# Attention and feed-forward on one Trainium2 core: the first stage and first chunk in one written order, scores taken from the loaded keys, block sums in column quarters

## The chip, the cores and the metric

The kernel runs on one core of a Trainium2 chip. The core has five engines that run side by side: PE (TensorE, matrix multiplications), DVE (VectorE), ACT (ScalarE), POOL (GpSimd) and SP, which here only issues transfers (DMA). The metric is device microseconds of one launch. The median of three runs before is 675.34 us (675.28 to 675.90).

## The reference

```python
# q, k, v: (4 batches, 8 heads, 768 positions, 64), fp32; w_in, w_out arrive as 64-bit floats
k_sum = k.reshape(B, H, 24, 32, D).max(axis=3)          # maxima of blocks of 32
v_sum = v.reshape(B, H, 24, 32, D).mean(axis=3)         # means of blocks of 32
scores_l = where(|i - j| < 16, scale * q @ k.T, -1e9)   # a band around the diagonal
scores_s = scale * q @ k_sum.T + log(32)
a = softmax(concat(scores_l, scores_s))
x = (a @ concat(v, v_sum)).reshape(B * S, H * D)        # 3072 x 512
h = x @ w_in                                            # 512 -> 2048
out = where(h > 0, h, exp(min(h, 0)) - 1) @ w_out       # 2048 -> 512
```

## The kernel before

Two heads make a pair, so there are four pairs of each batch. A "unit" is 256 positions (four windows of 64 queries) of one pair. A window sees 96 keys and 24 block maxima, so its scores are 128 x 120: 64 queries of each of two heads. For each unit PE makes the scores (`unit_scores`, L386), DVE adds the mask and finds the row minimum of the negated scores (L118), ACT takes the exponentials (L122), DVE makes the reciprocal of the sum (L124, L125), POOL multiplies (L126), PE transposes (L132), ACT or DVE copies the result (L133), PE multiplies with the values (L139), and `take_x` splits the result into a rounded part `xh` (ACT, L152) and the rest `xl` (DVE, L153).

The feed-forward part takes chunks of 512 positions, six in all, and runs 96 iterations n: chunk c = n // 16, slice f = n % 16 of the 2048 hidden columns. `layer1` (L412) makes `h` from twelve products; ACT takes exp (L415), DVE makes the ELU (L416, L417), ACT rounds it to `gh` (L420), POOL makes the rest `gl` (L421); `layer2` (L432) of iteration n is issued in iteration n + 1. Iterations n = 0 to 79 also carry 40 units, one for two iterations: an even n has the scores of the next unit and the transposes of the present one, an odd n its values. In the first chunk scores, transposes and values share one PSUM bank, "a0".

The weights are 32 tiles, (1, f) of w_in and (2, f) of w_out, 512 KB each as 64-bit floats. Each is turned into two fp32 tiles by `convert`: POOL shifts the low words (L98), ACT scales the high words into PSUM (L96), DVE joins them (L100, L103), ACT rounds (L106), POOL subtracts (L107).

The first stage, `first_units`, makes the first chunk's x: 512 positions of all four pairs. It loads q as blocks with zeros (`q_t`) and k whole (`kn`), copies the windows of k and its maxima into `k_t`, and multiplies full 128 x 128 tiles (L289). The block means of v come from twelve products with 512 columns (L298). A scheduler orders the first stage on PE, DVE, ACT and POOL; only SP is written by hand there. In the loop PE and SP are written by hand, and the scheduler places the rest. Six weights are converted ahead of the loop, two more in each iteration of the first chunk. For the next batch, `summary` loads k and v of a whole pair (`n`, 384 KB) and reduces them on DVE (L361); `means` (L376) is eight products.

SP keeps at most eight transfers open: the ninth waits for the first. `load_unit` issues six transfers of 40 to 144 KB (L322, L328, L332, L340, L341).

## Time and profile before

| | |
|---|---|
| median of three runs | 675.34 us |
| the profiled execution | 675.21 us |
| its span, first to last instruction | 673.4 us |
| PE busy | 649.0 us, 96% of the span |
| DVE, ACT, POOL busy | 274.5, 280.2, 249.4 us |
| chain that ended last | PE 85%, DMA 6%, POOL 3% |

The busy times are sums over the span. What matters for a change at the start is the start alone, so the views of the first 105 us are read apart from the rest: the timeline of PE (when an iteration's first `layer1` starts), the groups of instructions in one window (count, mean, idle time before and what ended it), and the windows view (busy time, granted clock and bytes moved in each stretch).

### The profile page before, as it was taken

The page shows a single profiled execution, that of the slowest core. Times are in us where ns is not written, and L with a number is a line of the kernel's source. Part 1 is how long each engine was busy: PE and PEld are TensorE (multiplying, and loading weights), DVE is VectorE, ACT ScalarE, POOL GpSimd, SP SyncE. Part 2 cuts the span into 40 slices and gives each one's busy share as a digit, 9 for nine tenths or more (in the row PEclk, how much of TensorE's full clock was granted, in tenths as well). Part 3 has the DMA queues.
Part 4 walks back from the last instruction along what each step waited for, and adds up shares of the span by engine and source line. Part 5 has one row for each costly group of instructions (what it writes and reads, how often), then busy time and mean ns, then how long its engine had stood idle before and what let it go on. Part 6 is the DMA issues. An engine that isn't in the chain of part 4 may idle for free.

```text
span 673.4 us, 10291 instructions
## 1 busy us (share of the span) xinstructions
PE 649.0 (96%) x3688; PEld 527.6 (78%) x3688; DVE 274.5 (41%) x866; ACT 280.2 (42%) x754; POOL 249.4 (37%) x269
## 2 busy tenths in 40 slices
PE   7769999999999999999999999999999999999996
PEld 5457777888888888888888888888888888888885
DVE  6676987772333543222322553232322222311111
ACT  5565666674334334433433433343434333322222
POOL 7466787983223222322222232223223222122221
PEclk9969999999999999999999999999999999999999
DMA  9979982113112341411212443112312100100001
GB/s 293 303 192 323 336 277 70 36 46 96 47 32 79 100 131 41 126 32 32 58 36 55 137 128 79 47 43 55 94 32 60 32 1 1 63 0 1 0 1 63
DMA packets 88146, 60.21 MB, mean 89 GB/s; under 512 B 48544, under 2 KB 80544, under 8 KB 88096
## 3 DMA queue, kind: packets, MB, share of 16 engines
q1 hardware_dynamic: 84784, 53.66, 28.8%
q10 hardware_dynamic: 3312, 5.90, 2.4%
q8 instruction: 29, 0.48, 0.3%
q14 instruction: 21, 0.17, 0.1%
HBM read 52.46 MB, written 6.29 MB: 87 GB/s over the span
## 4 chain that ended last, share of the span: by engine, by line
PE 85%; DMA 6%; POOL 3%; SPq 2%; DVE 1%; ACT 1%; issue 1%; ACTq 0%; POOLq 0%
PE h L412 37%; PE o L432 37%; PE s L386 5%; DMA raw_w<-in_w_out_dram 4%; PE o_ps L139 3%; PE t_ps L132 2%; DMA v<-in_v_dram 1%; DMA raw_w<-in_w_in_dram 1%; POOL raw_w L98 1%; POOL w L107 1%; ACT sm L122 1%; SPq L158 1%; POOL gl L421 1%; POOL sm L126 0%; SPq L250 0%
## 5 line engine op out<-in xcount | busy, mean ns | idle before, releaser
L412 PE MATMUL h<-xh,w 128*128 128x512 f32 x768 | 262.0, 402 | 1.5 <-ACT xh L152 1.5
L421 POOL TENSOR_TENSOR gl<-e,gh 128x512 fp32r<-128x512 f32 x96 | 123.7, 1289 | 206.3 <-issue 114.0
L432 PE MATMUL o<-w,gh 128*128 128x512 f32 x768 | 196.1, 394 | 0.0
L412 PEld LDWEIGHTS h<-xh,w 128*128 128x128 f32 x768 | 144.6, 188 | 33.1 <-ACT xh L152 1.7
L432 PEld LDWEIGHTS o<-w,gh 128*128 128x128 f32 x768 | 141.2, 188 | 27.8 <-DVE ot L453 0.4
L416 DVE TENSOR_SCALAR e<-e 128x512 f32<-128x512 f32 x96 | 49.2, 512 | 260.6 <-ACT e L415 260.6
L412 PE MATMUL h<-xl,w 128*128 128x512 f32 x384 | 150.3, 391 | 0.3 <-DVE xl L153 0.3
L415 ACT ACTIVATE e<-h 128x512 f32<-128x512 f32 x96 | 57.3, 597 | 205.0 <-PE h L412 204.8
L126 POOL TENSOR_TENSOR sm<-sm,z 128x480 f32<-128x480 f32 x48 | 48.1, 1003 | 161.7 <-ACT gh L420 130.1
L432 PE MATMUL o<-w,gl 128*128 128x512 f32 x384 | 105.4, 389 | 0.0
L420 ACT CAST gh<-e 128x512 fp32r<-128x512 f32 x96 | 59.0, 614 | 67.3 <-DVE e L417 65.9
L122 ACT ACTIVATE sm<-sm,mx 128x120 f32<-128x120 f32 x192 | 73.6, 385 | 30.9 <-DVE mx L118 28.2
L432 PEld LDWEIGHTS o<-w,gl 128*128 128x128 f32 x384 | 72.0, 188 | 15.2 <-POOL gl L421 0.2
L412 PEld LDWEIGHTS h<-xl,w 128*128 128x128 f32 x384 | 72.5, 189 | 13.3 <-DVE xl L153 0.6
L417 DVE SCALAR_TENSOR_TENSOR e<-h,e 128x512 f32<-128x512 f32 x96 | 66.1, 689 | 1.9
L107 POOL TENSOR_TENSOR w<-cv,w 128x512 fp32r<-128x512 f32 x32 | 42.0, 1321 | 12.1 <-ACT w L106 11.4
L386 PEld LDWEIGHTS s<-kw,qbd 128*128 128x128 f32 x320 | 42.5, 194 | 5.0 <-DVE xl L153 2.0
L386 PE MATMUL s<-kw,qbd 128*128 128x120 f32 x320 | 43.0, 278 | 1.6 <-DVE xl L153 1.6
L118 DVE CUSTOM_DVE_ANT_0 sm<-s,mask 128x120 f32<-128x120 f32 x192 | 42.5, 277 | 4.5 <-PE s L289 3.3
L153 DVE TENSOR_TENSOR xl<-o_ps,xh 128x256 fp32r<-128x256 f32 x48 | 20.0, 422 | 56.6 <-ACT xh L152 56.5
L122 ACT ACTIVATION_READ_ACCUMULATOR sm<-sm,mx 128x1 f32 x192 | 36.1, 188 | 0.0
L133 ACT COPY pt<-t_ps 120x512 f32<-120x512 f32 x44 | 25.7, 585 | 22.6 <-PE t_ps L132 22.2
(69 smaller groups left out, 390.1 us busy)
## 6 DMA issues: line engine op xcount, KB each, us to landing
raw_w<-in_w_in_dram SPq DMA_DIRECT2D x16, 512.0 KB, 6.6
raw_w<-in_w_out_dram SPq DMA_DIRECT2D x16, 512.0 KB, 8.4
qbd<-in_qT_dram SPq DMA_DIRECT2D x80, 64.0 KB, 2.3
out_dram<-ot ACTq DMA_DIRECT2D x20, 256.0 KB, 3.8
kw<-in_kT_dram SPq DMA_DIRECT2D x28, 144.0 KB
vw<-in_v_dram SPq DMA_DIRECT2D x28, 144.0 KB, 3.5
n<-in_kT_dram SPq DMA_DIRECT2D x16, 192.0 KB, 2.5
n<-in_vT_dram SPq DMA_DIRECT2D x16, 192.0 KB, 2.5
```

The lines of the kernel that those rows point to most:

```text
L107: nc.gpsimd.tensor_tensor(out=w[:, 1, :], in0=cv, in1=w[:, 0, :].bitcast(F32), op=ALU.subtract)
L118: low = nc.vector.tensor_tensor_reduce(out=sm[:, t, :], in0=s_ps[:, t, :], in1=m, scale=-scale, scalar=3.0e38, op0=ALU.add, op1=ALU.min, a ...
L122: exp = nc.scalar.activation(out=sm[:, t, :], in_=sm[:, t, :], func=AF.Exp, bias=mx[:, t, :], scale=-1.0, accum_out=z[:, t, :])
L126: mul = nc.gpsimd.tensor_tensor(out=sm, in0=sm, in1=z.broadcast_to([P, UW, KC]), op=ALU.mult)
L386: nc.tensor.matmul(s_ps[:, t, :], qbd[u % 2][:, t, :], kw[p][:, t, :], start=True, stop=True)
L412: nc.tensor.matmul(h_ps, w[:, a, cols], bb[:, cc, :], start=(k == 0), stop=(k == 3 * NCC - 1))
L415: exp = nc.scalar.activation(out=e, in_=h_ps, func=AF.Exp)
L416: nc.vector.tensor_scalar(out=e, in0=e, scalar1=1.0, scalar2=-1.0, op0=ALU.min, op1=ALU.add)
L417: elu = nc.vector.scalar_tensor_tensor(out=e, in0=h_ps, scalar=0.0, in1=e, op0=ALU.max, op1=ALU.add)
L420: nc.scalar.copy(out=gh, in_=e)
L421: low = nc.gpsimd.tensor_tensor(out=gl, in0=e, in1=gh.bitcast(F32), op=ALU.subtract)
L432: nc.tensor.matmul(o_acc[c][s], a[:, s * P:(s + 1) * P], w[:, bb, :], start=first and f == 0, stop=last and f == NF - 1)
```

## The change

Scores of the first stage no longer need the blocks `q_t` and `k_t`: each head of each window is one product of 64 x 64 queries with 96 keys straight from `kn`, and one with 24 maxima from `ks`; the two heads of a pair stand in the two halves of the rows and of the output. That is 32 products for a pair in place of 8. The block sums become 24 products of 128 columns, each pair in its own quarter of the output columns of PE (`tile_position=(0, p * BLK)`), and `means` likewise. The first stage and the first sixteen iterations stand in one written order on all five engines. `convert` becomes a generator of four parts (POOL; ACT; DVE; ACT and POOL) that are called half an iteration apart; three weights are converted in the first stage, two in each iteration after it. The weights are loaded in the order of their use, and the loads of units 0 and 1 stand between weights. Summaries are loaded in one iteration and reduced in the next, at a fixed place. From the second chunk on the scheduler places DVE, ACT and POOL as before.

```diff
+    order = [(1, 0)]
+    for f in range(1, NF):
+        order += [(1, f), (2, f - 1)]
+    order.append((2, NF - 1))
+    todo, loads = list(order), list(order)
...
-    def convert(key, turn):
...
+    def convert(tag="a1"):
...
+        key = todo.pop(0)
...
-        sh = psum.tile([P, WC], F32, tag="a1", name="sh")
+        nc.gpsimd.tensor_scalar(out=lo_w, in0=lo_w.bitcast(U8)[:, :, 3], scalar1=1 / 32, scalar2=-31 / 64,
+                                op0=ALU.mult, op1=ALU.add)
+        yield
+        sh = psum.tile([P, WC], F32, tag=tag, name="sh")
         bits = sh.bitcast(U32)
-        with tc.issue_after(turn[1]):
-            nc.scalar.mul(out=sh, in_=hi_w.bitcast(F32), mul=2.0 ** -112)
-        with tc.issue_after(turn[2]):
-            nc.gpsimd.tensor_scalar(out=lo_w, in0=lo_w.bitcast(U8)[:, :, 3], scalar1=1 / 32, scalar2=-31 / 64,
-                                    op0=ALU.mult, op1=ALU.add)
+        nc.scalar.mul(out=sh, in_=hi_w.bitcast(F32), mul=2.0 ** -112)
+        yield
         nc.vector.scalar_tensor_tensor(out=bits, in0=bits, scalar=3, in1=lo_w,
                                        op0=ALU.logical_shift_left, op1=ALU.bitwise_or)
...
                                        op0=ALU.bitwise_and, op1=ALU.bitwise_or)
+        yield
         w = wts.tile([P, 2, WC], F32R, tag=f"w{key[0]}_{key[1]}", name=f"w{key[0]}_{key[1]}")
...
-            load(key)
+        load_more(1)
...
-        for key in order[2:10]:
-            load(key)
...
+        load_more(3)
+        load_unit(0)
+        load_more(6)
+        load_unit(1)
+        load_more(9)
...
+        def scores(p):
+            q_p = qn[p // 2][:, p % 2]
             for th in range(2):
-                s_ps = psum.tile([P, UW, KC], F32, tag=f"o{(2 * p + th) % NSUB}", name="s")
-                for t in range(UW):
-                    w = th * UW + t
-                    done = nc.tensor.matmul(s_ps[:, t, :], q_t[p][:, w, :], k_t[p][:, w, :], start=True, stop=True)
...
-            if p == 1:
-                ps = psum.tile([P, row], F32, tag="a1", name="vsps")
-                with tc.issue_after(done.ins):
-                    for j in range(2 * NTH):
-                        nc.tensor.matmul(ps[KB:KB + BLK, :], mean[:, BLK - per * j:2 * BLK - per * j],
-                                         vn[j // 2][:, j % 2, :], start=(j == 0), stop=(j == 2 * NTH - 1),
-                                         tile_position=(0, KB))
...
+                banks_of[p, th] = psum.tile([P, UW, KC], F32, tag=f"o{(2 * p + th) % NSUB}", name="s")
+            for cols in (slice(0, KB), slice(KB, KC)):
+                for th in range(2):
+                    for t in range(UW):
+                        w = th * UW + t
+                        for h in range(2):
+                            rows = slice(h * D, (h + 1) * D)
+                            right = kn[p][rows, w * QW:w * QW + KB] if cols.start == 0 else ks[rows, p, :]
+                            nc.tensor.matmul(banks_of[p, th][rows, t, cols], q_p[rows, w * QW:(w + 1) * QW], right,
+                                             start=True, stop=True)
...
+        def sums():
+            ps = psum.tile([P, P], F32, tag="a1", name="vsps")
+            for j in range(2 * NTH):
+                for p in range(NP):
+                    nc.tensor.matmul(ps[p * BLK:(p + 1) * BLK, :], mean[:, BLK - per * j:2 * BLK - per * j],
+                                     vn[j // 2][:, j % 2, p * P:(p + 1) * P],
+                                     start=(j == 0), stop=(j == 2 * NTH - 1), tile_position=(0, p * BLK))
+            nc.scalar.copy(out=vs, in_=ps)
...
+        maxima(0)
+        scores(0)
+        maxima(1)
+        low_exp(0, 0)
+        scores(1)
+        low_exp(0, 1)
+        maxima(2)
+        norm(0, 0)
+        scores(2)
+        low_exp(1, 0)
+        norm(0, 1)
+        low_exp(1, 1)
+        maxima(3)
+        norm(1, 0)
+        scores(3)
+        low_exp(2, 0)
+        norm(1, 1)
...
+        low_exp(2, 1)
+        trans(0, 0, dve)
...
+        one = convert(tag="o3")
+        next(one)
+        put_means(0, 1, v_t[1], pool)
+        norm(3, 1)
+        next(one)
+        put_means(0, 2, v_t[2], act)
...
+        list(one)
+        next(two)
+        vals(2, 0)
+        vals(2, 1)
+        three = convert(tag="o3")
+        next(three)
+        vals(3, 0)
+        vals(3, 1)
+        unit_scores(0, 0)
+        next(two)
+        low = unit_low(0)
+        list(two)
+        next(three)
+        unit_exps(0, low)
+        next(three)
+        for p in range(NP):
+            put_means(0, p, vw[p])
+        load_more(12)
+        return three
...
-        ps = psum.tile([P, row], F32, tag=bank(c), name="vsps")
-        for p in range(NP):
-            nc.tensor.matmul(ps[KB:KB + BLK, p * P:(p + 1) * P], vst_all[b][:, p, :], ident, start=True, stop=True,
-                             tile_position=(0, KB))
...
+        ps = psum.tile([P, P], F32, tag=bank(c), name="vsps")
+        for p in range(NP):
+            nc.tensor.matmul(ps[p * BLK:(p + 1) * BLK, :], vst_all[b][:, p, :], ident, start=True, stop=True,
+                             tile_position=(0, p * BLK))
...
-    with tc.manual_schedule(engines={mybir.EngineType.SP}):
-        end = first_units()
-        load_unit(0)
-        load_unit(1)
-        for p in range(NP):
-            put_means(0, p, vw[p])
-        load_more(12)
-    convert_more(6, end)
...
-    unit_scores(0, 0)
-    with tc.manual_schedule(engines={mybir.EngineType.PE, mybir.EngineType.SP}):
-        for n in range(NCH * NF):
...
+    def slot_a(n, c):
+        u, odd = divmod(n, 2)
+        if not odd and u + 1 < len(units):
+            unit_scores(u + 1, c)
+            if u + 2 < len(units):
...
+    with tc.manual_schedule(engines=set(engines.values())):
+        late = first_units()
+        got = {}
+        e = None
+        this = begin_next()
+        for n in range(NF):
+            u, odd = divmod(n, 2)
+            h_ps = layer1(0, n)
+            next(this, None)
+            ahead = begin_next()
+            if n > 0:
+                split(0, n - 1, e)
+            next(this, None)
+            if n > 0:
+                evacuate()
+            list(late)
+            if not odd:
+                unit_norm(u)
+            for key in [(n - 1, 0), (n - 2, 1)]:
+                if key in got:
+                    summary(1, key[0], (kT, vT)[key[1]], got.pop(key))
+            slot_a(n, 0)
+            if n < NP:
+                got[n, 0] = load_summary(1, n, kT, spares[0][n])
+            if 1 <= n < NP + 1:
+                got[n - 1, 1] = load_summary(1, n - 1, vT, spares[1][n - 1])
+            load_more(12 + 3 * (n + 1))
+            late, this = this, ahead
+            next(this, None)
+            ahead = begin_next()
+            e = exp_of(h_ps)
+            next(this, None)
+            list(late)
+            if not odd:
+                low = unit_low(u + 1)
+            elu(e, h_ps)
+            if odd:
+                unit_exps(u + 1, low)
+            if n > 0:
+                layer2(0, n - 1)
+            late, this = this, ahead
+            evacuate = slot_b(n, 0)
+        list(late)
+        split(0, NF - 1, e)
+        evacuate()
+        unit_norm(NF // 2)
...
-            if n > 0:
-                layer2(*divmod(n - 1, NF))
-            if u < len(units):
-                (unit_values if odd else unit_transposes)(u, c)
...
-            if c == 0:
-                load_more(12 + 3 * (n + 1))
-                convert_more(6 + 2 * (n + 1), turn)
```

The order of DVE in the loop, up to the first reduction of a summary (`ks<-n`) and after it; `raw_w1_3` is the loaded tile of weight (1, 3), `e` the ELU. Before:

```order
L416 TENSOR_SCALAR e_643<-e_643 128x512
L417 SCALAR_TENSOR_TENSOR e_643<-h_630,e_643 128x512
L361 TENSOR_REDUCE ks_676<-n_680 128x24
L124 TENSOR_SCALAR z_662<-z_662 128x4
L125 RECIPROCAL z_662<-z_662 128x4
L416 TENSOR_SCALAR e_727<-e_727 128x512
L417 SCALAR_TENSOR_TENSOR e_727<-h_714,e_727 128x512
L361 TENSOR_REDUCE ks_676<-n_735 128x24
L100 SCALAR_TENSOR_TENSOR sh_696<-sh_696,raw_w1_3_188 128x512
L103 SCALAR_TENSOR_TENSOR cv_700<-raw_w1_3_188,sh_696 128x512
```

The same place on DVE after the change:

```order
L510 TENSOR_SCALAR e_731<-e_731 128x512
L511 SCALAR_TENSOR_TENSOR e_731<-h_680,e_731 128x512
L110 SCALAR_TENSOR_TENSOR sh_766<-sh_766,raw_w1_3_193 128x512
L113 SCALAR_TENSOR_TENSOR cv_774<-raw_w1_3_193,sh_766 128x512
L440 TENSOR_REDUCE ks_716<-n_720 128x24
L110 SCALAR_TENSOR_TENSOR sh_791<-sh_791,raw_w2_2_201 128x512
L113 SCALAR_TENSOR_TENSOR cv_797<-raw_w2_2_201,sh_791 128x512
L510 TENSOR_SCALAR e_794<-e_794 128x512
L511 SCALAR_TENSOR_TENSOR e_794<-h_753,e_794 128x512
```

The first reduction stands between two conversions now, and the second iteration's ELU stands behind it. Before, weight (1, 3) came behind the ELUs of both iterations.

SP around the loads of the first two units, before (raw_w: weights, qbd, kw, vw: one unit's queries, keys and values, vs: the block means):

```order
L76 DMA raw_w1_4_192<-in_w_in_dram 128x4x128
L76 DMA raw_w2_4_194<-in_w_out_dram 128x512
L322 DMA qbd0_70<-in_qT_dram 64x4x64 x2
L328 DMA kw0_72<-in_kT_dram 128x3x96
L332 DMA vw0_76<-in_v_dram 96x3x128
L340 DMA kw0_72<-in_kT_dram 128x80
L341 DMA vw0_76<-in_v_dram 80x128
L322 DMA qbd1_71<-in_qT_dram 64x4x64 x2
L328 DMA kw1_73<-in_kT_dram 128x3x96
L332 DMA vw1_77<-in_v_dram 96x3x128
L340 DMA kw1_73<-in_kT_dram 128x80
L341 DMA vw1_77<-in_v_dram 80x128
```

And after:

```order
L81 DMA raw_w1_1_179<-in_w_in_dram 128x4x128
L81 DMA raw_w2_0_181<-in_w_out_dram 128x512
L395 DMA qbd0_70<-in_qT_dram 64x4x64 x2
L401 DMA kw0_72<-in_kT_dram 128x3x96
L405 DMA vw0_76<-in_v_dram 96x3x128
L413 DMA kw0_72<-in_kT_dram 128x80
L414 DMA vw0_76<-in_v_dram 80x128
L81 DMA raw_w1_2_189<-in_w_in_dram 128x4x128
L81 DMA raw_w2_1_191<-in_w_out_dram 128x512
L81 DMA raw_w1_3_193<-in_w_in_dram 128x4x128
L395 DMA qbd1_71<-in_qT_dram 64x4x64 x2
L401 DMA kw1_73<-in_kT_dram 128x3x96
```

Unit 0 is issued behind three weights instead of ten, and three more weights stand between it and unit 1; six more then precede unit 2, where before there were two.

## Rows read from the trace of the kernel before

**Rows 1.** windows: length, busy us (count): PE, PEld, DVE, ACT, POOL; PEclk, DMA share, GB/s

```profile
5.00:45.80 40.80, 28.80 (x229) 22.08 (x229) 28.29 (x113) 23.65 (x87) 25.05 (x42) 0.89 0.99 274
...
60.90:105.00 44.10, 41.14 (x241) 32.97 (x237) 39.28 (x78) 27.85 (x67) 34.75 (x37) 1.00 0.95 292
105.00:673.40 568.40, 563.22 (x3142) 461.95 (x3140) 193.98 (x634) 217.85 (x572) 176.36 (x159) 1.00 0.20 54
```

**Rows 2.** timeline of PE in the loop: start, us; last: idle before

```profile
45.76 0.77 PE L412 MATMUL h<-xh,w 128*128 128x512 f32 x1
...
97.67 1.06 PE L376 MATMUL vsps<-ident,vst 128*32 128x128 f32 x8 [1.40 <-ACT pt L133]
...
104.95 0.50 PE L412 MATMUL h<-xh,w 128*128 128x512 f32 x1
...
107.80 1.04 PE L386 MATMUL s<-kw,qbd 128*128 128x120 f32 x8
...
111.46 0.63 PE L132 MATMUL t_ps<-ident,sm 128*120 128x128 f32 x4
111.85 0.47 PE L412 MATMUL h<-xh,w 128*128 128x512 f32 x1
...
118.15 0.50 PE L412 MATMUL h<-xh,w 128*128 128x512 f32 x1
```

**Rows 3.** DVE groups, 5 to 45.8 us: count | busy us, mean ns | idle

```profile
L118 DVE CUSTOM_DVE_ANT_0 sm<-s,mask 128x120 f32<-128x120 f32 x32 | 7.1, 277 | 3.3 <-PE s L289 3.3
L277 DVE TENSOR_REDUCE ks<-kn 128x24 f32<-128x768 f32 x4 | 3.8, 948 | 0.0
L124 DVE TENSOR_SCALAR z<-z 128x4 f32<-128x4 f32 x8 | 3.7, 463 | 0.8 <-ACT sm L122 0.8
...
L133 DVE COPY pt<-t_ps 120x512 f32<-120x512 f32 x4 | 2.7, 684 | 5.2 <-PE t_ps L132 5.2
...
L125 DVE RECIPROCAL z<-z 128x4 f32<-128x4 f32 x8 | 1.4, 174 | 0.2
```

**Rows 4.** timeline of PE: scores, block sums and values of the first stage

```profile
7.21 3.74 PE L289 MATMUL s<-k,q 128*128 128x120 f32 x16 [2.23 <-DVE k L281]
...
15.95 5.51 PE L298 MATMUL vsps<-vn,mean 128*32 128x512 f32 x12
...
29.60 1.62 PE L139 MATMUL o_ps<-pt,v 120*64 120x64 f32 x48
```

**Rows 5.** timeline of DVE: the first reduction

```profile
5.00 0.95 DVE L277 TENSOR_REDUCE ks<-kn 128x24 f32<-128x768 f32 x1
```

**Rows 6.** groups of DVE in the loop, 45.8 to 98.7 us

```profile
L103 DVE SCALAR_TENSOR_TENSOR cv<-raw_w,sh 128x512 uint32<-128x512 uint32 x14 | 9.6, 685 | 0.8
L100 DVE SCALAR_TENSOR_TENSOR sh<-sh,raw_w 128x512 uint32<-128x512 uint32 x13 | 9.0, 694 | 3.2 <-ACT sh L96 3.0
L416 DVE TENSOR_SCALAR e<-e 128x512 f32<-128x512 f32 x7 | 6.4, 913 | 1.9 <-ACT e L415 1.9
L417 DVE SCALAR_TENSOR_TENSOR e<-h,e 128x512 f32<-128x512 f32 x7 | 4.8, 685 | 0.1
L118 DVE CUSTOM_DVE_ANT_0 sm<-s,mask 128x120 f32<-128x120 f32 x20 | 4.4, 275 | 1.1 <-PE s L386 1.1
L361 DVE TENSOR_REDUCE ks<-n 128x24 f32<-128x768 f32 x4 | 3.8, 951 | 1.6 <-DMA n<-in_kT_dram 1.6
...
L153 DVE TENSOR_TENSOR xl<-o_ps,xh 128x256 fp32r<-128x256 f32 x5 | 2.1, 416 | 0.0
```

**Rows 7.** windows picked by what was loaded in them: last column GB/s

```profile
2.00:16.00 14.00, 10.44 (x37) 7.70 (x36) 9.71 (x45) 8.08 (x29) 11.12 (x33) 1.00 1.07 326
18.00:26.00 8.00, 6.92 (x37) 3.76 (x34) 3.23 (x13) 2.97 (x13) 1.25 (x2) 1.00 1.18 227
28.00:36.00 8.00, 5.14 (x93) 4.48 (x94) 7.87 (x30) 5.39 (x26) 6.61 (x8) 1.00 1.07 375
38.00:48.00 10.00, 7.12 (x52) 6.18 (x52) 7.57 (x21) 5.68 (x14) 6.07 (x6) 0.55 0.46 93
```

More of the change, by code (lines that the diff above doesn't have):

```diff
@@ L301, in first_units @@
-        with tc.issue_after(ends[2][0]):
-            nc.vector.tensor_copy(out=vs[KB:KC], in_=ps[KB:KC])
-        for p in range(NP):
-            put_means(0, p, v_t[p], (nc.vector, nc.gpsimd)[p % 2].tensor_copy)
-        for p in range(NP):
-            for th in range(2):
-                pt = pts[p][:, th]
-                transposes(sms[p][:, th], "h", pt, (nc.scalar.copy, nc.vector.tensor_copy)[th], bufs=2)
-                take_x(values(v_t[p], th * UW, pt, ("a0", "o0", "o1", "o2")[2 * (p % 2) + th]), th, p)
+        load_more(3)
@@ new lines, in first_units @@
+        vals(0, 1)
+        put_means(0, 3, v_t[3], pool)
+        two = convert()
+        next(two)
+        next(one)
+        trans(3, 0, act)
+        vals(1, 0)
+        trans(3, 1, dve)
+        vals(1, 1)
+        list(one)
[7 more added lines that the diff above has]
+        unit_scores(0, 0)
+        next(two)
+        low = unit_low(0)
+        list(two)
+        next(three)
@@ L491, in attn_elu_ffn @@
+    with tc.manual_schedule(engines={engines["PE"], engines["SP"]}):
+        for n in range(NF, NCH * NF):
             c, f = divmod(n, NF)
             u, odd = divmod(n, 2)
-            turn = layer1(c, f)
-            if u < len(units):
-                if not odd and u + 1 < len(units):
-                    unit_scores(u + 1, c)
-                    if u + 2 < len(units):
-                        load_unit(u + 2)
+            h_ps = layer1(c, f)
+            e = exp_of(h_ps)
+            turn = elu(e, h_ps)
+            split(c, f, e)
+            slot_a(n, c)
+            if not odd and u + 1 < len(units):
+                unit_exps(u + 1, unit_low(u + 1))
+                unit_norm(u + 1)
```

260 lines of the change are left out of this document (139 added, 121 removed).

## The prediction

> **What bounds the kernel now.** I read the windows first, to see where PE is not full. From 105 us to the end PE is busy 563.2 of 568.4 us [rows 1], so nothing that only frees another engine there can change the time. Between 5 and 105 us it is not: 28.8 of 40.8 us in the first stage, and 41.1 of 44.1 later [rows 1]. The timeline of PE gives the two marks that I use. S0 is the start of the first `layer1`, 45.76 us; S8 is the start of iteration 8, 104.95 us [rows 2]. From S8 on an even iteration takes 111.85 - 104.95 = 6.9 us and an odd one 118.15 - 111.85 = 6.3, 13.2 for two [rows 2]. Without waits S0 to S8 would be: iteration 0 without `layer2` (the 2.85 us that a layer takes, 107.80 - 104.95) 4.05, then 6.3, then three times 13.2, and the 1.06 of `means` [rows 2]: 51.0 us. It was 59.2. So 8.2 us are lost in the loop, and the 45.76 us ahead of it are mostly not PE work. The change can only gain by a smaller S8, plus a trifle in two later `means`. All that follows works out the new S8; the time is 675.21 (this execution's own time; the median of the runs is 0.1 higher) minus what S8 comes earlier.
>
> **First stage.** Before, DVE waited 5.2 us for transposes and 3.3 for scores there [rows 3], and PE waited for the blocks `k_t` (2.23 us ahead of the first scores [rows 4]). The change removes the copies into `q_t` and `k_t` from ACT, DVE and POOL, and puts the steps of different pairs one behind the other on every engine. DVE then has no long gap left, and its own work is the sum. It starts at 5.0 us, when the first keys are there [rows 5]; the change does not move that. Then: 4 reductions of 0.95 = 3.8; 32 minima, 7.1 busy; 8 sums and reciprocals, 0.46 + 0.17 each = 5.1; 6 copies of transposes at 0.68 = 4.1 [rows 3]; 8 rests `xl` at 0.42 = 3.3; one conversion, 0.69 + 0.69 = 1.4 [rows 6]. Together 24.8, which ends at 29.8. Walking the written order through with these durations I find two gaps: 0.4 us for the first scores and some 1.1 for the last pair's transposes, which wait for POOL's multiplication behind the copies of the block means. So S0 is about 31.3 in place of 45.76. ACT and POOL have less to do than DVE and lie beside it; if their steps are late, DVE's copies are late with them.
>
> The scores cost more instructions: 32 products for a pair in place of 8, 64 on PE where 16 were. The trace has no product of 64 rows. Bounds for one pair: the values, two heads in two halves of the columns, took 1.62 us for 48 instructions of 64 columns, 34 ns each [rows 4]; by columns 51 ns for 96, and 34 at least for 24, so 32 x 85 ns = 2.7 us. If the two heads do not overlap and PE runs as in the first scores, 3.74 us for 16 instructions of 120 columns [rows 4], 1.95 ns a column, it is 32 x (187 + 47) ns = 7.5 us. DVE has 6.2 us a pair (24.8 / 4) and hides the lower bound. I take 2.7, since the values are nearest in kind. Less than the old 3.74 would gain nothing, because DVE is behind it.
> The Trainium skill, "TensorEngine Tiling (Array Packing)", section "Gotcha 1: PSUM Pressure", says that different row tiles cannot access the same PSUM bank at once; the two heads here stand in different rows and write one bank. By it they would run one after the other, the rival "heads one after the other" below; rows 4 have different columns and the same rows, and cannot tell.
>
> The block sums keep their column count: 48 instructions of 128 columns against 12 of 512 that took 5.51 us [rows 4]. Between a quarter of that, 1.4 us, if four column quarters run together, and 5.5 if none do. The 34 ns of the values speak for overlap; I take 2. PE has room for either, because the transposes behind them wait for POOL and DVE.
>
> **Loads.** The queue before fell to 93 GB/s between 38 and 48 us, while SP issued two units and four block means in a row; with weights alone it moved 375, with the 512-byte rows of `v_t` 227 [rows 7]. The new order puts weights between the units, so I drop that hole. What must land by when: unit 0 ahead of S0, and the first summary, which iteration 1 reduces at a fixed place on DVE. That one stands behind 4.2 MB of keys, queries and values (at 326 to 375 GB/s [rows 7]: 12.9 to 11.2 us), 12 weights, 6.3 MB at 375 (16.8), three units, `v_t` and the block means, 3.3 MB at 227 (14.4), and itself, 0.4 MB (1.0). From 2 us that makes 45.4 to 47.1; I take 46. By the same rates unit 0 is there at about 28, in time, and the next pair of summaries behind unit 3 at 46 + 4.7 MB more = 60.8.
>
> **Iterations 0 to 4.** DVE again, with these prices [rows 3, 6]: conversion 1.4, minima 0.9, z 0.6, ELU 0.91 + 0.69 = 1.6, reduction 0.95, `xl` 0.4. Iteration 0 has four conversions (two left of the three early ones, two more), two sets of minima, z and the ELU, 9.6 and 0.7 of waits on ACT's and POOL's parts: it ends at 41.6. Iteration 1: one conversion to 43.0, then DVE stands until the summary lands at 46, and behind it are queued one conversion and the ELU: 46 + 0.95 + 1.4 + 1.6 = 50.0. `layer2` of that iteration waits for it, and so do the next unit's scores, since `xl` frees their bank. Iteration 2: two conversions, `xl`, z, two reductions, minima, ELU, 8.2, to 58.2. Iteration 3: conversion to 59.6, wait to 60.8, two reductions, conversion, ELU: 65.7. Iteration 4 up to the minima 6.6: 72.3. The transposes use the same bank and come then, 0.4 us, so iteration 5 starts at 72.7. PE waits for 4 to 5 us in iterations 0 and 1 on the way. Before, the granted clock was 0.55 of 2.4 GHz, so mostly 1.2 GHz, between 38 and 48 us, where PE waited [rows 7]; if it falls again, a `layer1` takes up to 2.85 us more, but DVE comes last there all the same, so I add nothing. From there on DVE has 5 to 6 us of work for each iteration and PE 6.3 to 6.9, and the loads are ahead: 72.7 + 6.3 + 6.9 + 6.3 and 0.5 for `means` (between 0.3, four together, and 1.06) give S8 = 92.7.
>
> **The sum.** 104.95 - 92.7 = 12.3 us earlier. Two later `means` in the full part save 0 to 0.8 each; with 0.5, 1.1 together. 675.2 - 12.3 - 1.1 = 661.8, say 662. Removed from the sum at no cost: three weights fewer are converted ahead of the loop, since DVE's sum has them in iteration 0.
>
> **Rivals.**
> "Loop at PE's pace": DVE's overlaps are better than my prices and the summaries land early, so that only PE counts: 31.3 + 4.05 + 6.3 + 39.6 + 0.5 = 81.8, 23.2 us earlier, 651. For it: the reduction's wait disappears if the load is 3 us early, and DVE works ahead of need by more than half an iteration. Against it: DVE was busy 39.3 of 44.1 us with nearly the same work [rows 1], and iterations 2 and 4 have 8.2 us of it against PE's 6.9. A half-way case gives 656.
> "Loads decide": if they go at the 292 GB/s of 60.9 to 105 us throughout [rows 1], the first summary (14.1 MB) lands at 2 + 48.3 = 50.3, 4.3 us later, and every later step with it: 666, to 669 if the hole stays.
> "Heads one after the other": at the rate of the scores in the loop, 1.04 us for 8 of 120 columns [rows 2] or 1.08 ns a column, a pair takes 32 x (104 + 34) ns = 4.4 us; the fourth pair's scores end at 5 + 17.6 = 22.6 where DVE wants them at 18.8, so S0 is 4 us later: 666.
> "Slower": the same, and PE stays at the slower rate of the first scores through the stage. 7.5 us a pair end at 35 instead of 18.8, 16 us later, more than the 13.4 of the sum: 678. It turns from about 6.8 us a pair. For it: the first two pairs before ran so [rows 4]. Against it: PE works from the first scores on with few gaps now.
> "The order does nothing": every engine waits at each written step for another, S0 comes at 42 or later, and the time is 672 to 675.
>
> **How the numbers follow.** The forecast 0.45 (its own range 658 to 666), loop at PE's pace or half-way 0.22, loads decide 0.14, heads one after the other 0.10, the order does nothing 0.05, slower 0.04. A measurement of this kernel can tell about 0.2% from no change, 1.4 us. Faster takes all but the last and a part of the one before it: 0.94; same 0.02; slower 0.04. For 8 in 10 the range goes from 652.5, inside the case at PE's pace, to 668.5, which takes in slow loads and serial heads.
>
> **What would show it.** S0 near 31 and S8 near 93 in the timeline of PE. In the first stage DVE without gaps of over 1 us. In iteration 1 DVE waiting some 3 us for the summary's load, and PE waiting for the ELU, for `xl` or for the bank in iterations 1 to 4, not later. Scores at about 2.7 us for a pair, sums at 2. No hole in the bytes moved from 38 to 48 us. I am wrong if S0 is over 36 (then the first stage, by PE or by POOL), if S8 - S0 is near 51 (then DVE did not bound), or if PE waits in iterations 9 to 15.

## The result, and the profile after

The changed kernel took 666.83 us (median of 4 runs, 666.13 to 667.99), the kernel before 675.31 beside it: a ratio of 0.9875 (95% interval 0.9858 to 0.9892), 1.25% faster. I had said 662, with 652.5 to 668.5 around it. The direction and the range held; the size was 8.5 us in place of 13.4. The ratios are of fast runs alone, while the medians of "unit 1 first" and of the table's last row each take in one slow run.

The profiled execution took 666.64 us, its span is 664.9. The windows of the changed kernel, to be read against [rows 1] and [rows 7] (length, busy us of PE, PEld, DVE, ACT and POOL, granted clock, DMA share, GB/s), first by stage, then the stretches of the loads:

```profile
5.00:20.00 15.00, 13.40 (x320) 12.37 (x320) 13.91 (x84) 12.05 (x63) 8.32 (x20) 1.00 1.10 327
20.00:37.00 17.00, 10.86 (x164) 8.77 (x164) 13.54 (x34) 11.63 (x32) 12.26 (x14) 0.98 1.03 259
37.00:46.00 9.00, 7.66 (x29) 6.55 (x30) 4.67 (x14) 4.34 (x9) 6.52 (x8) 0.65 0.96 311
46.00:60.00 14.00, 9.18 (x50) 7.29 (x49) 7.92 (x14) 5.46 (x16) 6.63 (x7) 0.77 1.07 347
...
105.00:664.90 559.90, 555.05 (x3104) 454.64 (x3103) 187.63 (x618) 211.97 (x564) 171.10 (x156) 1.00 0.20 54
```

```profile
2.00:24.00 22.00, 19.54 (x368) 15.45 (x366) 18.36 (x95) 16.90 (x73) 14.33 (x37) 1.00 1.06 314
24.00:51.00 27.00, 20.39 (x183) 16.89 (x184) 14.81 (x41) 14.04 (x39) 17.36 (x20) 0.87 1.03 284
...
38.00:48.00 10.00, 8.92 (x43) 7.19 (x43) 3.77 (x13) 5.42 (x15) 7.19 (x8) 0.74 1.02 309
```

PE is full behind 105 us, as before. The loads of 38 to 48 us, 93 GB/s in [rows 7], now move 309. But PE is busy only 7.66 of 9.0 us from 37 to 46 and 9.18 of 14.0 from there to 60, at a granted clock of 0.65 and 0.77.

The timeline of PE (start, duration, what it runs, and in brackets the idle time just before it) gives the marks. The rows begin with the scores of the second pair and the block sums; the `layer1` rows at 29.84, 41.10, 48.37, 62.24 and 97.90 open iterations 0, 1, 2, 3 and 8:

```profile
7.57 1.53 PE L287 MATMUL s<-kn,qn 64*64 64x96 f32 x32
...
9.83 1.53 PE L287 MATMUL s<-kn,qn 64*64 64x96 f32 x32
...
16.19 1.52 PE L312 MATMUL vsps<-vn,mean 128*32 128x128 f32 x48
...
29.84 0.47 PE L500 MATMUL h<-xh,w 128*128 128x512 f32 x1
...
37.25 2.03 PE L464 MATMUL s<-kw,qbd 128*128 128x120 f32 x8 [4.42 <-DMA kw<-in_kT_dram]
40.37 1.08 PE L149 MATMUL t_ps<-ident,sm 128*120 128x128 f32 x4 [1.08 <-DVE mx L130]
41.10 0.78 PE L500 MATMUL h<-xh,w 128*128 128x512 f32 x1
...
48.37 0.50 PE L500 MATMUL h<-xh,w 128*128 128x512 f32 x1
```

```profile
56.22 2.06 PE L464 MATMUL s<-kw,qbd 128*128 128x120 f32 x8 [4.82 <-DVE xl L170]
57.95 3.20 PE L528 MATMUL o<-w,gh 128*128 128x512 f32 x8
...
62.24 0.47 PE L500 MATMUL h<-xh,w 128*128 128x512 f32 x1
...
72.87 1.15 PE L464 MATMUL s<-kw,qbd 128*128 128x120 f32 x8 [1.35 <-DVE xl L170]
...
93.98 0.43 PE L454 MATMUL vsps<-ident,vst 128*32 128x128 f32 x8
...
97.90 0.50 PE L500 MATMUL h<-xh,w 128*128 128x512 f32 x1
```

So S0 came at 29.84 in place of 45.76, 15.9 us earlier [rows 2]. S8 came at 97.90 in place of 104.95, only 7.05 earlier: of the 15.9 us the loop gave 8.9 back. Behind S8 the kernel needs 664.9 - 97.90 = 567.0 us, where it was 673.4 - 104.95 = 568.45; the two later `means` are in that 1.45. Together 8.5.

The loop's 68.1 us from S0 to S8 are made up like this. Without waits it would be 50.5 (the 51.0 of the prediction with `means` at 0.5). The idle times on these rows and one more (0.60 us ahead of the transposes of iteration 4) come to 4.42 + 1.08 + 4.82 + 1.35 + 0.60 = 12.3. And behind the two long ones PE ran at half its clock for a while: the scores took 2.03 and 2.06 us where they take 1.05 to 1.15, the transposes 1.08 for 0.6, and `layer1` of iteration 1 and the `layer2` issued in iteration 2 a microsecond more each; some 4.5 us in all. That makes 67.3 of the 68.1. What held PE is on DVE. Its timeline:

```profile
42.30 0.69 DVE L113 SCALAR_TENSOR_TENSOR cv<-raw_w,sh 128x512 uint32<-128x512 uint32 x1
51.02 0.95 DVE L440 TENSOR_REDUCE ks<-n 128x24 f32<-128x768 f32 x1 [8.03 <-DMA n<-in_kT_dram]
...
53.74 0.69 DVE L511 SCALAR_TENSOR_TENSOR e<-h,e 128x512 f32<-128x512 f32 x1
...
55.75 0.42 DVE L170 TENSOR_TENSOR xl<-o_ps,xh 128x256 fp32r<-128x256 f32 x1
```

At 42.99 DVE is through with a conversion; its next written step is the reduction of the first summary, and that load lands at 51.0. For 8.03 us it stands, with a conversion, the ELU of iteration 1 and the `xl` of the unit behind it. PE finishes `layer1` of iteration 2 at 51.4, needs that `xl` for the bank of the next scores, and gets it at 56.2.

### The profile page after: what moved, and what is told of

Its sections match the earlier page's. It is cut to its first block, busy times and chain, and to the rows that moved or that the text cites. A ratio compares the mean times of both kernels' runs of the same rounds, so it can differ in the third digit from the quotient of the medians.

```text
span 664.9 us, 10778 instructions
## 1 busy us (share of the span) xinstructions
PE 642.8 (97%) x3916; PEld 525.1 (79%) x3916; DVE 265.3 (40%) x856; ACT 275.3 (41%) x750; POOL 244.1 (37%) x263
## 3 DMA queue, kind: packets, MB, share of 16 engines
q1 hardware_dynamic: 82960, 53.66, 29.2%
## 4 chain that ended last, share of the span: by engine, by line
PE 90%; DMA 6%; DVE 2%; SPq 1%; issue 1%; POOL 0%; ACT 0%; DVEq 0%; POOLq 0%
PE h L500 39%; PE o L528 38%; PE s L464 5%; PE o_ps L156 4%; DMA raw_w<-in_w_in_dram 3%; PE t_ps L149 3%; DMA raw_w<-in_w_out_dram 2%; PE s L287 1%; DMA vw<-in_v_dram 1%; DMA n<-in_vT_dram 1%; PE idle L224 1%; SPq L81 0%; DVE cv L113 0%; DVE sh L110 0%; DVE sm L130 0%
## 5 line engine op out<-in xcount | busy, mean ns | idle before, releaser
L510 DVE TENSOR_SCALAR e<-e 128x512 f32<-128x512 f32 x96 | 43.7, 455 | 253.7 <-ACT e L506 253.6
L156 PEld LDWEIGHTS o_ps<-pt,vw 120*64 120x64 f32 x640 | 21.9, 137 | 14.1 <-ACT gh L517 9.2
```

Source lines behind the costliest of these rows:

```text
L156: nc.tensor.matmul(o_ps[h * D:(h + 1) * D, t * QW:(t + 1) * QW], v_t[0:KC, w0 + t, h * D:(h + 1) * D], pt[0:KC, t, h * QW:(h + 1) * QW], s ...
L510: nc.vector.tensor_scalar(out=e, in0=e, scalar1=1.0, scalar2=-1.0, op0=ALU.min, op1=ALU.add)
```

## The experiments

All are edits of the changed kernel and compute the same. The table gives the starts of iterations 0, 1, 3 and 8 in the one profiled execution of each kernel; the ratios are to the kernel before on the same chip.

| kernel | median us | ratio, 95% interval | it. 0 | it. 1 | it. 3 | it. 8 |
|---|---|---|---|---|---|---|
| before | 675.3 | 1 | 45.76 | 54.64 | 67.78 | 104.95 |
| changed | 666.83 | 0.9875 (0.9858 to 0.9892) | 29.84 | 41.10 | 62.24 | 97.90 |
| order left to the scheduler | 682.08 | 1.0092 (1.0072 to 1.0112) | 51.90 | 62.98 | 78.22 | 111.55 |
| unit 1 first | 668.67 | 0.9891 (0.986 to 0.9921) | 30.44 | 41.65 | 63.20 | 100.16 |
| summaries later | 661.81 | 0.9792 (0.9763 to 0.9822) | 30.90 | 41.00 | 56.16 | 94.65 |
| both | 662.59 | 0.9808 (0.9784 to 0.9832) | 30.27 | 42.52 | 57.44 | 95.62 |
| fewer weights ahead | 659.56 | 0.9765 (0.9743 to 0.9787) | 30.21 | 40.76 | 57.84 | 91.18 |
| fewer weights, summaries later | 659.74 | 0.9774 (0.975 to 0.9798) | 30.36 | 40.62 | 55.24 | 90.27 |
| all five edits | 660.11 | 0.9767 (0.975 to 0.9785) | 29.94 | 38.09 | 53.66 | 88.35 |
| half an iteration | 658.05 | 0.9753 (0.9738 to 0.9767) | 30.14 | 39.52 | 53.82 | 88.42 |
| the same, means in a row | 657.82 | 0.9753 (0.9737 to 0.977) | 29.78 | 38.65 | 53.83 | 87.24 |
| the same, one weight between the units | 657.64 | 0.9735 (0.9721 to 0.975) | 30.42 | 39.00 | 53.03 | 87.97 |
| products one after the other | 667.43 | 0.9878 (0.984 to 0.9916) | 35.15 | 45.26 | 61.91 | 100.78 |
| half an iteration, products one after the other | 662.37 | 0.9813 (0.9796 to 0.9829) | 35.45 | 44.02 | 58.29 | 91.75 |

### Is it the written order that makes the first stage short?

```diff
-    with tc.manual_schedule(engines=set(engines.values())):
+    with tc.manual_schedule(engines={engines["PE"], engines["SP"]}):
```

> In the first stage and chunk 0 only PE and SP keep the written order; DVE, ACT and POOL are ordered by the scheduler again. Scores from the loads, the sums in quarters and the order of the loads stay. Theory "the written order makes the first stage short": iteration 0 starts at 35 to 42 in place of 29.8, with gaps of over 1 us on DVE ahead of it; the time depends on where the scheduler puts the summaries, 664 to 672. Rival "scores from the loads make it short": iteration 0 starts at 30 to 32, and the time is 664 to 667.

Iteration 0 came at 51.90, 22 us later than with the order and 6 later than in the kernel before: worse than either theory allowed, but the first by kind. The new products and the new order of the loads without the written order on DVE, ACT and POOL make the kernel slower by 0.9%. PE keeps its written order here, so the run does not show what a scheduler that orders PE as well would reach. The timeline of POOL shows the place (rows as above):

```profile
26.49 0.65 POOL L103 TENSOR_SCALAR raw_w<-raw_w 128x512 uint32<-128x512 uint8 x1 [5.36 <-DMA raw_w<-in_w_in_dram]
...
28.93 1.93 POOL L144 TENSOR_TENSOR sm<-sm,z 128x480 f32<-128x480 f32 x2
...
34.00 0.64 POOL L103 TENSOR_SCALAR raw_w<-raw_w 128x512 uint32<-128x512 uint8 x1 [2.13 <-DMA raw_w<-in_w_out_dram]
...
42.05 3.22 POOL L174 COPY v<-vs 24x1024 f32<-24x1024 f32 x3
```

The scheduler put the first step of a conversion ahead of the normalisations of the first stage, five times from 26 to 36 us; each stands for a weight's load (5.36 us at the first, 2.13 at the fourth), and `put_means`, which the values of the first stage need, came at 42.05. A load that is late holds up all that is queued behind the instruction that waits for it, here on POOL; in the changed kernel it is the same thing on DVE.

### Is it the first summary that holds the loop?

Two waits stand out in the changed kernel: PE's 4.42 us for unit 1's keys in iteration 0, DVE's 8.03 for the summary in iteration 1. One edit for each, and both:

```diff
         load_unit(0)
+        load_unit(1)
         load_more(6)
-        load_unit(1)
         load_more(9)
```

```diff
-            for key in [(n - 1, 0), (n - 2, 1)]:
+            for key in [(n - 2, 0), (n - 3, 1)]:
```

Unit 1 first:

> The loads of unit 1 stand ahead of three weights (1.5 MB, at 300 GB/s 5.2 us) in place of behind them; nothing else moves. In the changed kernel PE stood 4.4 us for unit 1's keys in iteration 0, and DVE 8.0 us for the first summary in iteration 1. Theory "the summary decides": the keys land some 5 us earlier and iteration 1 starts at 36 to 38 in place of 41.1, but the summary lands at 51 as before, DVE's wait grows to 11 or 12 us, iteration 3 starts at 62 as before, and the time is 666 to 667.5. Rival "each wait counts by itself": iteration 3 starts 4 to 5 us earlier, 661 to 663.

Summaries later:

> Each summary of chunk 0 is reduced one iteration later; its load stays where it is. Theory "the summary decides": DVE does not wait 8.0 us in iteration 1, PE's wait of 4.8 us for xl in iteration 2 falls under 1.5 and with it the slow clock there (2 us), iteration 3 starts at 56 to 58 in place of 62.2, and the time is 660 to 662.5. Rival "the next load takes its place": unit 2's keys, or the second pair of summaries, are as late as the first summary was; iteration 3 starts at 60 to 62 and the time is 664 to 667.

Both:

> Both edits. Theory "the summary decides": with the summary out of the way the wait for unit 1's keys counts as well, so the pair saves more than the sum of the two: 3 to 5 us under the second edit alone, 656 to 659, iteration 1 at 36 to 38, iteration 3 at 51 to 54. Rival "the queue as a whole decides": all that is loaded up to iteration 4 comes at the rate of the queue whatever the order, and a later load (unit 2, the summaries) takes back what unit 1 gained: within 1 us of the second edit alone.

Reducing the summaries an iteration later gave 0.8%, about 5.6 us, with iteration 3 at 56.16: the first theory, and its number. Loading unit 1 first gave nothing, and not as that theory had said: iteration 1 did not come earlier at all (41.65), and DVE's wait for the summary grew to 9.07 us, not to 11 or 12. PE's and POOL's timelines of the kernel with unit 1 first show what took its place:

```profile
33.26 1.04 PE L464 MATMUL s<-kw,qbd 128*128 128x120 f32 x8
40.91 1.08 PE L149 MATMUL t_ps<-ident,sm 128*120 128x128 f32 x4 [6.61 <-DVE mx L130]
```

```profile
35.62 0.64 POOL L103 TENSOR_SCALAR raw_w<-raw_w 128x512 uint32<-128x512 uint8 x1 [1.86 <-DMA raw_w<-in_w_in_dram]
36.92 0.65 POOL L103 TENSOR_SCALAR raw_w<-raw_w 128x512 uint32<-128x512 uint8 x1 [0.66 <-DMA raw_w<-in_w_out_dram]
...
38.89 0.98 POOL L144 TENSOR_TENSOR sm<-sm,z 128x480 f32<-128x480 f32 x1
```

The keys are there (the scores of unit 1 run at 33.26 without a wait), but now the weights behind them come late. POOL stands for two of them (1.86 and 0.66 us), its multiplication for the unit is queued behind that, DVE's conversion of the first of them waits for POOL's part of it, the minima of unit 1 stand behind that on DVE, and PE's transposes wait 6.61 us for both. With the summaries out of the way the edit gave nothing either (0.9808 against 0.9792): here the rival's number was right. Of the loads that iteration 0 needs, one came late in either order.

### Or is it what is loaded ahead of need?

Then the remedy is not order but amount. Two weights are converted in an iteration; the changed kernel has 12 loaded ahead of the loop and three more in each iteration, in the same queue as units and summaries.

```diff
-        load_more(9)
+        load_more(7)
...
-        load_more(12)
+        load_more(7)
...
-            load_more(12 + 3 * (n + 1))
+            load_more(9 + 2 * n)
```

Fewer weights ahead:

> Fewer weights are loaded ahead of need: 7 in place of 12 ahead of iteration 0, then 9 + 2n in place of 12 + 3(n + 1) in iteration n; nothing else moves. The loads before had moved unit 1 ahead of three weights without a gain, since conversions then waited for the weights. Theory "weights that are loaded too early hold up the summary": five weights (2.6 MB, 8.7 us at 300 GB/s) no longer stand ahead of the first summary, which lands at 42 to 44 in place of 51; DVE's wait in iteration 1 is under 1 us, iteration 3 starts at 56 to 57, and the time is 656 to 661. Rival "the queue as a whole decides": the conversions of iterations 1 to 4 wait for their weights instead, and the time is 663 to 667.

Fewer weights, summaries later:

> Fewer weights ahead, and each summary reduced one iteration later as well. If the summary's landing is what the first of the two mends, the second adds little: within 2 us of fewer weights alone, 655 to 661. If the summaries are still late in iterations 2 to 4 (two a time, 0.8 MB), it adds 2 to 5 us.

Three numbers took 1.1% off, 7.4 us. (The interval overlaps with that of the later summaries, so which of the two single edits is worth more is open.) S8 came at 91.18: S0 to S8 is 61.0 in place of 68.1, so most of what the loop had given back is there again, with the first stage untouched. The first summary was reduced at 47.10 after a wait of 4.46 us:

```profile
47.10 0.95 DVE L440 TENSOR_REDUCE ks<-n 128x24 f32<-128x768 f32 x1 [4.46 <-DMA n<-in_kT_dram]
```

That is 3.9 us earlier, not the 7 to 9 that I had worked out, because the queue ran low. From 36 to 42 us (columns as above) the first row, this kernel, moves 133 GB/s, the second, the changed kernel, 278:

```profile
36.00:42.00 6.00, 4.00 (x15) 3.58 (x16) 5.24 (x17) 3.00 (x6) 4.49 (x7) 0.56 0.50 133
```

```profile
36.00:42.00 6.00, 3.66 (x14) 3.34 (x15) 4.63 (x16) 2.65 (x5) 4.02 (x6) 0.54 0.95 278
```

Behind unit 1 one weight was queued in place of six ahead of unit 2, and then SP issued the row of four block means (3.51 us) and the six small loads of unit 2, until 43.5. A part of the rival is there too: POOL stood 4.48 us for a weight, until 48.99. So the time is the theory's, two of its steps (the landing, and DVE's wait of under 1 us) are not. To reduce the summaries later as well added nothing (0.9774 against 0.9765), so their landing no longer decides the time.

### What is left of it

All the edits together, with two more: the conversions from the fourth weight on start an iteration later, and the four DMAs that copy block means to unit rows are spread over iterations 0 to 5.

```diff
-        this = begin_next()
+        this = iter(())
...
-            ahead = begin_next()
+            ahead = begin_next() if n > 0 else iter(())
```

All five edits:

> Fewer weights ahead, summaries one iteration later, unit 1 ahead of the weights, the conversion of each weight from the fourth on one iteration later, and the four copies of block means to unit rows by DMA spread over iterations 0 to 5 in place of one row of four (3.5 us of SP). Theory "each load when it is needed": no wait of over 1.5 us is left in the loop, iteration 0 starts at 30 and iteration 8 at 82 to 86, and the time is 651 to 655. Rival "the bytes up to iteration 4 are too many at 300 GB/s in any order": PE still waits 5 us or more in iterations 0 to 5, 656 to 661.

Half an iteration:

> As the run with all five edits of loads and conversions, but the conversions are half an iteration later in place of a whole one. There iteration 8 started at 88.35, 2.8 us ahead of the run with fewer weights alone, yet iterations 9 to 16 took 6.8 to 7.1 us each in place of 6.9 and 6.3 in turn, and PE waited some 0.5 us for POOL's part of a conversion in several of them. Theory "the conversion came too late": iterations 9 to 16 take 13.2 us a pair again, iteration 8 starts at 85 to 88, 653 to 657. Rival "weights in iteration 0 are waited for again": iteration 1 starts at 40 or later, 658 to 661.

The same, means in a row:

> As the half-iteration version, but the four copies of block means stand in a row behind the first stage again, as in the changed kernel (3.5 us of SP's time without a large load behind them). Theory "SP's issue leaves the queue empty": the bytes moved fall under 150 GB/s for 4 us or more between 36 and 46 us, unit 2 and the first summary land 2 to 3 us later, and the time is 1.5 to 4 us over that version. Rival "the queue has enough in it": within 0.8 us of it.

The same, one weight between the units:

> As the half-iteration version with the four copies of means in a row, but the fourth weight is loaded between unit 0 and unit 1 in place of behind unit 1. In the half-iteration version POOL stood 2.5 us for that weight in iteration 0, with the unit's multiplication queued behind it and PE's transposes behind that (4 us). Theory "one weight at the wrong place": the weight lands 2 to 3 us earlier, unit 1's keys 1 to 2 us later, iteration 1 starts at 37 to 38.5 in place of 39.5 and 38.7, and the time is 655.5 to 657.3. Rival "the loads of iteration 0 come at the same end in any order": PE waits for unit 1's keys in its place, iteration 1 starts at 38.5 to 40, 657.3 to 659.

All five edits took 660.11 us, in the rival's range and not in the theory's. S8 came at 88.35, not at 82 to 86; that is still 2.8 us ahead of fewer weights alone, yet the time was the same. The gain went behind S8, where the seven iterations 8 to 14 took 48.0 us in place of 46.1. PE now waited there for a weight's last part:

```profile
99.15 1.88 PE L527 MATMUL o<-w,gh 128*128 128x512 f32 x7 [0.46 <-POOL w L118]
```

It is 659.0 - 88.35 = 570.7 us behind S8, where fewer weights alone took 657.8 - 91.18 = 566.6. Waits for weights make 0.7 of these 4.1 us in the rows, waits for other engines 1.5; the rest was not traced. Half an iteration (the second change of that diff undone) mended more than half of it: 656.7 - 88.42 = 568.3, and two iterations took 13.1 us again, as the theory said. But its 658.05 us lie in the rival's range, though iteration 1 began before 40. The means in a row cost nothing (0.9753 both), so my theory that SP's issue leaves the queue empty fell, at this place, where weights are queued ahead of it: from 36 to 42 us the first row below (means in a row) moves 253 GB/s, the second (spread) 273, not under 150.

```profile
36.00:42.00 6.00, 4.08 (x12) 3.44 (x13) 4.80 (x15) 2.80 (x5) 5.64 (x7) 0.52 0.99 253
```

```profile
36.00:42.00 6.00, 3.21 (x10) 2.75 (x11) 4.56 (x14) 3.62 (x7) 5.55 (x8) 0.73 1.05 273
```

One weight between the units gave the lowest ratio, 0.9735, but its interval overlaps with those of the versions before it, up to fewer weights alone (0.9743 to 0.9787): the rival's number (657.3 to 659) holds. That the edits made after fewer weights gain anything more is not shown clear of noise. This version beats both kernels, by 2.7% and 1.4%, with edits of what is loaded and converted when. From S0 to S8 it still needs 57.6 us where 50.5 would do without waits; 8.6 of them are iteration 0, which needs 4.05. But the rival's mechanism is not there: PE waited only 0.17 us for unit 1's keys and POOL for no weight. PE's long wait is 3.57 us for DVE's minima of unit 1, which stand behind two conversions in DVE's written order (33.1 to 37.2). To put the minima ahead of them was not tried.

### Do neighbouring products overlap, and what was the first stage worth?

```diff
-                for th in range(2):
-                    for t in range(UW):
-                        w = th * UW + t
-                        for h in range(2):
+                for h in range(2):
+                    for th in range(2):
+                        for t in range(UW):
+                            w = th * UW + t
...
-            for j in range(2 * NTH):
-                for p in range(NP):
+            for p in range(NP):
+                for j in range(2 * NTH):
```

In the changed kernel:

> The scores of a pair take all products of the first head and then all of the second, in place of the two heads in turn, and the block sums one column quarter after the other in place of the four in turn: the same instructions in another order. Theory "neighbours in other rows or columns of the array overlap": a pair takes 4.0 to 4.9 us in place of 2.5, the sums 4.5 to 5.6 in place of 1.5, DVE waits for scores, and iteration 0 starts 3 to 5 us later; the time follows by less, since the loads decide behind it: 666 to 670. Rival "the instructions are short because they have few columns": both take what they took, and the time is 666 to 667.5.

In the half-iteration version:

> As the half-iteration version, but scores head by head and block sums quarter by quarter. In the changed kernel that edit made iteration 0 start 5.3 us later and the time only about 1 us longer, since the loads came last there anyway. Theory "the loads took back what the first stage gained": with the loads in order of need a first stage that is 5 us longer costs 3 to 6 us. Rival "the loop takes it back for another reason": 0 to 2 us here as well.

With the heads in turn a pair's scores repeat every 9.83 - 7.57 = 2.26 us, and the block sums take 1.52. One after the other they take 15.77 - 12.22 = 3.55 (the rows are the 96-column products of a pair and the 24-column ones behind them) and 4.21:

```profile
12.22 2.12 PE L287 MATMUL s<-kn,qn 64*64 64x96 f32 x27
...
14.36 1.41 PE L287 MATMUL s<-ks,qn 64*64 64x24 f32 x25
...
15.77 2.11 PE L287 MATMUL s<-kn,qn 64*64 64x96 f32 x27
...
20.43 4.21 PE L312 MATMUL vsps<-vn,mean 128*32 128x128 f32 x48
```

So neighbours in other rows and columns of the array do overlap, by a factor of 1.6 for the scores and 2.8 for the sums. (3.55 and 4.21 us lie below the theory's 4.0 to 4.9 and 4.5 to 5.6.) What overlaps is not shown: it may be the products, or the weight loads of one with the products of another, since PEld is busy 14.97 of the 15.00 us from 5 to 20 us here and 12.37 in the changed kernel. The first stage needs the overlap: without it PE is busy for all of these 15.00 us (13.40 in the changed kernel), and iteration 0 starts at 35.15, 5.3 us later.

What those 5.3 us cost in the end tells less than I had hoped. With the loads as the change has them the ratio did not move (0.9878, but from two runs and with a wide interval); with fewer loads ahead it rose from 0.9753 to 0.9813, 4.1 us, as the theory said that the loads had taken back the gain. But S8 moved by 2.9 us in the one profiled execution and 3.3 in the other, which hardly differ. That the gain was given back to the loads is shown by the edits of the loads themselves, not by this pair.

## Why the prediction was right, and where it was not

**The first stage** came near what was worked out, in part by luck. I had 24.8 us of DVE's work and 1.5 of gaps; the groups of DVE up to the start of iteration 0 are, against [rows 3], with the last column the idle time ahead of them:

```profile
L130 DVE CUSTOM_DVE_ANT_0 sm<-s,mask 128x120 f32<-128x120 f32 x32 | 6.9, 272 | 0.1
L302 DVE COPY pt<-t_ps 120x512 f32<-120x512 f32 x6 | 4.1, 680 | 0.2 <-PE t_ps L149 0.2
L273 DVE TENSOR_REDUCE ks<-kn 128x24 f32<-128x768 f32 x4 | 3.8, 950 | 2.2 <-DMA kn<-in_kT_dram 2.2
L142 DVE TENSOR_SCALAR z<-z 128x4 f32<-128x4 f32 x8 | 3.3, 414 | 0.0
L170 DVE TENSOR_TENSOR xl<-o_ps,xh 128x256 fp32r<-128x256 f32 x8 | 3.1, 418 | 1.9 <-ACT xh L169 1.9
...
L143 DVE RECIPROCAL z<-z 128x4 f32<-128x4 f32 x8 | 1.4, 178 | 0.3
```

Minima 6.9 for 7.1, copies 4.1, reductions 3.8, z 3.3 + 1.4 for 5.1, rests 3.1 for 3.3. The 3.3 us for scores and 5.2 for transposes [rows 3] are 0.1 and 0.2. Behind the first keys the only gap of over 1 us is 1.08. I had one of 1.1, for the last pair's transposes; this one stands ahead of the last rests and ends with ACT's `xh`, so its size is right by luck. S0 was 1.5 us earlier than said, by two errors that partly cancel: DVE was busy 22.0 of the 25.1 us from its first reduction at 4.72, where the sum has 24.8 busy and 1.5 of gaps. Neighbouring durations overlap (minima of 0.28 us start 0.20 us apart), so adding them counts too much; and the gaps were 3.1 us, 0.60 of it for the second pair's keys. PE starts `layer1` at 29.84, as the last rest is written.

**Scores and sums** were 2.26 us a pair for 2.7, and 1.52 for 2.0, both near the lower bounds. The values of [rows 4] were the right neighbours for them. The rival "heads one after the other" is out. The rule it leaned on, in the Trainium skill, "TensorEngine Tiling (Array Packing)", section "Gotcha 1: PSUM Pressure", has different row tiles kept from one bank at the same time. Here two heads in different rows wrote one bank in 2.26 us a pair where the same products one head at a time took 3.55; they also write different partitions of it. So the price that I had read out of the rule, 4.4 us, did not come. That both wrote the bank at once is not shown: at the rate of a `layer1` (2.85 us for 12 x 512 columns) the 3840 columns of a pair would take 1.8 us, by this estimate less than 2.26 even one after the other.

**The order** is needed for any gain here: with DVE, ACT and POOL left to the scheduler the rest is a loss of 0.9%. The written order with the old products was not run. The rival "the order does nothing" had 0.05 and was as far off as could be.

**The loads** are the step that failed, by its size. The term is the landing of the first summary, "From 2 us that makes 45.4 to 47.1; I take 46"; it landed at 51.0. Up to 24 us the sum was right: 314 GB/s since 2 us make 6.9 MB, and my durations have about as much there. For the remaining 7.3 MB of the 14.2 I had counted the weights at 375 GB/s, the rate of a stretch with weights alone, and the units at 227 [rows 7]; that makes 22 to 23 us. It took 27, at 284 GB/s and a mean DMA share of 1.03; that is 7.7 MB, of which I put some 0.4, as an estimate, down to loads that SP issued behind the summary. So weights and units together were slower than my two rates. Whether the units' own rows are slower than the 227 of `v_t`, or the weights slower beside them, no run separates. The rival "loads decide" had taken 292 GB/s from a mixed stretch, gave 50.3 for the landing and 666 for the time, and was what happened; it had 0.14 and the forecast 0.45.

**The mechanism behind it** had the form that I predicted, later by nearly that one number. I said that DVE would stand in iteration 1 for the summary, with a conversion and the ELU behind it; it did, 8.0 us for 3.0. The ELU of iteration 1 ended at 53.74 + 0.69 = 54.4 for 50.0, and iteration 5 began 5.1 us late (77.77 for 72.7), iteration 8 5.2 (97.90 for 92.7). But the marks agree better than the account behind them. With the summaries an iteration later S8 came 3.25 us earlier, not 5.2, and PE still waited for units' keys (3.56 us in iteration 0, then 1.06 and 1.05): the first summary is not the only load that was late. The slower clock, which I had added nothing for, cost PE some 4.5 us in iterations 0 to 2; that it does not show in these marks, since DVE came last there, is argued and not tested.

**A wait that the sum did not have** is the 4.42 us for unit 1's keys: I had asked only for unit 0, and had PE's waits in iterations 0 and 1 from DVE's work; they came in 0 and 2. It was hidden: DVE stood only 1.07 us for those scores and was through with iteration 0 at 40.90 + 0.69 = 41.6 us, the very number of the prediction, but from a start 1.5 us sooner, so by 1.5 us more of waits than I had. The runs showed that the wait is no term by itself: moved, it comes back as a wait for weights.

**The rest.** PE waits in iterations 0, 2 and 4 and nowhere from 9 to 15, and S8 to the end is 1.45 us shorter for 1.1. "Loop at PE's pace", 0.22, needed the summaries three us early; even with the remedies above iteration 8 began at 87 to 88, not 81.8.

## What to carry to other kernels

When a first stage gets shorter, ask for each load behind it whether it lands earlier too; here 15.9 us were won ahead of the loop and 8.9 given back in it, because the queue delivered as before. Price such a queue by a stretch of the same mixture, not by the best rate of each kind, and look first at how much is loaded ahead of need, since three counts were worth 7.4 us where the whole change was worth 8.5. A step with a fixed place in an in-order engine that waits for a load holds all behind it, so place it by the landing, with an iteration to spare.

## What the runs showed of the hardware

Two things that I had not expected. The first is in [rows 3]: z, a `tensor_scalar` of four elements on each partition, took 463 ns there and 414 after, and I priced it so without asking why. The single rows show it: it took 0.16 us when POOL did nothing, and when POOL was in a long instruction it ended with it. Of DVE and POOL in the first stage:

```profile
10.89 0.48 DVE L142 TENSOR_SCALAR z<-z 128x4 f32<-128x4 f32 x1
...
13.15 0.16 DVE L142 TENSOR_SCALAR z<-z 128x4 f32<-128x4 f32 x1
...
14.23 0.45 DVE L142 TENSOR_SCALAR z<-z 128x4 f32<-128x4 f32 x1
...
19.86 0.95 DVE L142 TENSOR_SCALAR z<-z 128x4 f32<-128x4 f32 x1
```

```profile
10.36 0.99 POOL L144 TENSOR_TENSOR sm<-sm,z 128x480 f32<-128x480 f32 x1 [3.64 <-DVE mx L130]
...
13.67 0.99 POOL L144 TENSOR_TENSOR sm<-sm,z 128x480 f32<-128x480 f32 x1 [0.95 <-DVE z L143]
...
19.75 1.03 POOL L174 COPY v<-vs 24x1024 f32<-24x1024 f32 x1
```

10.89 + 0.48 = 11.37 and POOL's end is 10.36 + 0.99 = 11.35; 14.68 and 14.66; 20.81 and 20.78. The reductions, minima and reciprocals beside them kept their times. Eight of these sums cost 3.3 us where 8 x 0.16 would be 1.3, in a stage that DVE decides. The first step of the ELU, a `tensor_scalar` of 128 x 512, is stretched too: it took 0.42 us at 53.29 with POOL idle, 0.72 at 40.14 and 1.17 at 96.78, and the last two ended 0.28 and 0.29 us behind the POOL instruction that they met. [rows 6] has it at 0.91, and my sum took that price in each iteration. The Trainium skill, "SBUF — State Buffer", section "Who interferes with whom", says that DVE's `tensor_scalar` can take a port pair that it shares with GpSimd, and that whoever is later is then blocked until the other's instruction is done; the rows agree. To give z a place where POOL is idle, or another engine, was not tried.

The second is the price of a wait on PE beyond the wait itself: in and behind waits of 4.4 and 4.8 us (32.8 to 37.2 and 51.4 to 56.2) the granted clock was 0.50, 1.2 GHz, from 37 to 43 and from 54 to 60 us, and then 1.00, 2.4 GHz, again; the work at the lower level cost some 4.5 us more than at full clock. In the half-iteration version and the two rows of the table below it one such stretch is left, of 3 to 6 us between 37 and 43 us.
